# A first batch in a written order on four engines, with idle TensorE products, wider folds and one pool for the feed-forward operands

## The chip, the core and the metric

The kernel runs on one core of one Trainium2 chip. The time is device microseconds of one execution, as the median of three runs. The profile is one more execution, taken by the hardware profiler; its busy times, waits and clock are those of that execution.

Engines are named as in the profile: PE is TensorE, with PEld for its weight loads, DVE is VectorE, ACT is ScalarE, POOL is GpSimd, SP is SyncE, which here only issues DMAs.

## The reference

Eight batches, eight heads, 576 tokens of 64 values a head, 32 pack rows a head, all float32; the two weights come as float64.

```python
def sm_attn(qq, kk, vv):
    s = scale * np.matmul(qq, kk.transpose(0, 1, 3, 2))
    a = np.exp(s - np.max(s, axis=-1, keepdims=True))
    return np.matmul(a / (np.sum(a, axis=-1, keepdims=True) + 1e-09), vv)
p_packed = sm_attn(p, k, v)
x = sm_attn(q, p_packed, p_packed)          # then heads side by side: (8, 576, 512)
...
mixed = np.real(np.fft.fft(np.fft.fft(x, axis=1), axis=2))
u = x + mixed
un = (u - mean(u)) / np.sqrt(var(u) + 1e-06)    # over the 512 values of a token
return u + np.maximum(un @ w_ch1, 0.0) @ w_ch2  # 512 -> 2048 -> 512
```

## The kernel before, in words

**Products in three parts.** Nearly all products are made from operands split in a rounded high part (float32r) and the rest (`hi`, `lo`): `three` (line 240) issues high x high, high x low, low x high into one PSUM bank. A split is a rounding copy on ACT and a subtraction on DVE or POOL (`split`, line 100).

**Two kinds of work.** `front(b)` (line 245) makes one batch's `u`: for each half `g` of the heads, scores `s1` and their exponentials `e1` (letter `s` in the written order), turned by PE transposes (`t`), the packed rows `pp` (`p`), their transposes `ppT`, `pph`, `ppl` (`d`), the second scores `s2` (`q`), maximum and exponentials (`e`), mean and reciprocal (`m`), weights turned by DVE (`a`), the spectrum of the packed rows `gh`, `gl` from products `pg` with a table `basis` (`g`), sums and differences of the tokens `eo`, `f` (`f`, `r`: the folds) and their splits `fh`, `fl`, `xl`, `ol` (`h`). Then products `py`, their splits `yh`, `yl`, `yr`, products `pz` with the tables `tbh`, `tbl`, `tbr`, and products `px`; DVE adds them to `pe`, `qe` and four blocks of 128 tokens of `u` (`ubuf`, line 571). The 64 tokens left of a batch, its block R, go together with the next batch's.

`ffn` (line 659) is the feed-forward part of one tile of up to four blocks of 128 tokens: 16 steps `j`, each with 12 products `ph` (`up`, line 678, 128x512) and 12 products `acc` (`down`, line 695). Between them ACT makes `hh`, and DVE makes `hl` (line 685), which reads the one bank `ph`; so the next step's `ph` waits for `hl`. There are nine tiles, and 3456 such products of 512 columns (24 half-wide ones count as 12). While tile t runs, `front(t+1)` is dealt out over its half steps (`step`, line 776). Tiles 7 and 8 have no front beside them.

**Weights.** float64 chunks of 512 KB are fetched by SP into spare places (`fetch`, line 160) and made float32 by one ACT operation (line 181, "top") and two DVE operations (lines 182 and 183, "bits"). This happens once, in the first batch and in tile 0. Each tile splits all 32 chunks anew, into six buffers `wr`: ACT `wr_h` (line 101) and POOL `wr_l` (line 102).

**What sets the order.** For tiles 1 to 8 the code's order is kept on PE, DVE, ACT and POOL (`tc.manual_schedule`, `MANUAL`). The first batch and tile 0 are left to the tile framework's scheduler, which may reorder them when the program is built. `ORDER[0]` is the order in which the first batch's parts are handed to it; all of `front(0)`, block R too, stands before tile 0. SP's queue brings keys, tables, values, queries and the first weight chunks; the tables come as float32 through a staging place and are split on the chip (`load_base`, `load_tables`, lines 126 to 146).

**Waits between the two.** Tile 0 starts when the blocks of the first batch have been made, less their mean (`un`, line 628, DVE), turned (`untp`, line 635, PE) and split (`uh`, `ul`).

Of the kernel before, what the change touches and what calls it, by code (L numbers as in the profile page):

```python
# [38 lines left out]
ORDER = ("K0 I0 K1 B0 V0 V1 Q0 Q1 W0 W1 W2 W3 s0 t0 p0 d0 s1 t1 p1 q0 e0 d1 g0 q1 e1 m0 m1 a0 f0 r0 h0 a1 "  # L39
         "f1 r1 h1 g1 T0",  # L40
# [38 lines left out]
def tile_kernel(ctx, tc, kpT, qT, v, w1, w2, tabC, tabS, tabR, tabB, tabT, sel, ident_d, out):  # L79
# [3 lines left out]
    cpool = ctx.enter_context(tc.tile_pool(name="cpool", bufs=1))  # L83
    ld = ctx.enter_context(tc.tile_pool(name="ld", bufs=2))
# [15 lines left out]
    def split(hi, lo, src, lo_eng=None):  # L100
        nc.scalar.copy(hi, src)  # L101
        (lo_eng or nc.vector).tensor_tensor(lo, src, hi.bitcast(F32), ALU.subtract)  # L102
# [13 lines left out]
    ubuf = cpool.tile([P, NU, DM], F32, name="ubuf")  # L116
    stages = (STG0 + STG1 * 40)[:2 * NJ]
# [8 lines left out]
    def load_base():  # L126
        nc.sync.dma_start(sels, sel)
        st = load(tabB, [P, 2, N2], "st_base", "wst")
        h = work.tile([P, 2, N2], F32R, tag="tmp", name="base_h", bufs=3)
        nc.scalar.copy(h, st)  # L130
        nc.vector.scalar_tensor_tensor(basis, h.bitcast(F32), selC, st, ALU.mult, ALU.add)
        nc.sync.dma_start(turn, tabT)

    def load_tables():
        for t, d in enumerate((tabC, tabS)):
            st = load(d, [P, 1, KT], "st_tab", (t, 2))
            split(tbh[t], tbl[t], st[:, 0, :])
        st = work.tile([P, 2, 320], F32, tag="wst", name="st_tabr", bufs=2)
        nc.sync.dma_start(st[:101], tabR)
        for t in range(2):  # L140

            h = work.tile([P, DM], F32R, tag="tmp", name="tabr_h", bufs=3)
            nc.scalar.copy(h[:101, :320], st[:101, t, :])
            nc.vector.scalar_tensor_tensor(
                tbr[t][:101], h[:101, :320].bitcast(F32), selA[:101], st[:101, t, :], ALU.mult, ALU.add)
# [3 lines left out]
    sels = cpool.tile([P, 3], F32, name="sels")  # L149
    selA, selB, selC = (sels[:, i:i + 1] for i in range(3))  # L150
# [20 lines left out]
    def load_weights(j):  # L171

        for n, dst in enumerate((w1f, w2f)):
            if (j, n) not in fetched:
                fetch(j, n)
            st = fetched.pop((j, n))
            low, high = st[:, :, 0], st[:, :, 1]
            c = dst[:, j, :].bitcast(I32)


            nc.scalar.activation(c.bitcast(F32), high.bitcast(F32), AF.Prelu, scale=REBIAS, alpha=-2.0 ** 32)  # L181
            nc.vector.tensor_scalar(c, c, 3, None, ALU.logical_shift_left)
            nc.vector.scalar_tensor_tensor(c, low, 29, c, ALU.logical_shift_right, ALU.bitwise_or)
# [30 lines left out]
    def statistics(key):  # L214
        st, u = stat_of[key], u_of[key]
        nc.vector.tensor_scalar(st[:, 1:2], st[:, 0:1], 1.0 / DM, None, ALU.mult)  # L216
        meant[key] = steps[0] or 0

        def squares():
            junk = work.tile([P, DM], F32, tag="tmp", name="junk", bufs=3)  # L220
            nc.scalar.activation(junk, u, AF.Square, bias=st[:, 1:2], scale=-1.0, accum_out=st[:, 2:3])  # L221
# [5 lines left out]
        after(1, squares)  # L227
        after(2, deviation)
# [16 lines left out]
    def front(b):  # L245
# [31 lines left out]
        def scores(*gs):  # L277
# [11 lines left out]
            for g in gs:  # L289
# [31 lines left out]
        def packed(g):  # L321
# [15 lines left out]
            bd = work.tile([P, 4, D], F32, tag="tmp", name="bd", bufs=3)  # L337
            nc.gpsimd.tensor_tensor(bd, pp2[:, 0:1, :].to_broadcast([P, 4, D]),
                                    bmask.unsqueeze(2).to_broadcast([P, 4, D]), ALU.mult)

            def diagonals():
                bdh[g] = work.tile([P, 4 * D], F32R, tag="bdh", name="bdh")
                bdl[g] = work.tile([P, 4 * D], F32R, tag="bdl", name="bdl")
                split(bdh[g], bdl[g], bd.rearrange("p a d -> p (a d)"), nc.gpsimd)

            after(1, diagonals)

        def packed_parts(g):
# [10 lines left out]
            nc.vector.tensor_tensor(lo, tp[:, :P], hi.bitcast(F32), ALU.subtract)  # L359
# [44 lines left out]
        def values_spectrum(g):  # L404
# [6 lines left out]
            for t in range(2):  # L411
# [4 lines left out]
                x = work.tile([P, 2, N2], F32, tag="tmp", name="turned", bufs=3)  # L416
# [17 lines left out]
        def folded(g):
# [42 lines left out]

        def folded_parts(g):
# [3 lines left out]
            fh[g] = work.tile([P, FW], F32R, tag="fh", name="fh")  # L482
            nc.scalar.copy(fh[g], f)  # L483
# [4 lines left out]
            fl[g] = work.tile([P, FW], F32R, tag="fl", name="fl")  # L488
            nc.vector.tensor_tensor(fl[g], f, fh[g].bitcast(F32), ALU.subtract)
# [14 lines left out]
        yh, yl, yr = [], [], []  # L504
        for t, base in enumerate((0, FO)):
# [24 lines left out]
        def spectrum(t, par):  # L530

            pz = bank("pz")
            k0, off = (0, 0) if par is not None else (P, rows.start)
            pars = (0, 1) if par is None else (par,)
            for i, q in enumerate(pars):
                w = slice(KW * q + k0 - off, KW * q + k0 - off + P)
                three(pz[:, :N2], tbh[t][:, w], tbl[t][:, w], yh[t][:, q, :], yl[t][:, q, :], i == 0, False)
            k0 = KW * par if par is not None else k0
            nc.tensor.matmul(pz[:, :N2], tbr[t][:NRC[t], k0 - off:k0 - off + P], yr[t][:NRC[t]], start=False, stop=True)
            sb = work.tile([P, N2], F32, tag=f"spec{t}", name=f"spec{t}", bufs=1)  # L540
            nc.scalar.copy(sb, pz[:, :N2])
            return sb
# [13 lines left out]
        def halves(x):  # L556
            return x.rearrange("p (a c) -> p a c", a=2)
# [335 lines left out]
```

## Time and profile before

| | us |
|---|---|
| median of three runs | 1021.14 (1019.65 to 1021.65) |
| the profiled execution | 1019.84 |
| its span, first to last instruction | 1017.7 |
| PE, DVE, ACT, POOL busy in the span | 967.4, 611.7, 425.3, 469.4 |

A row of the timeline gives start, duration, engine, line, operation, output and inputs, and in square brackets how long the engine had been idle before it and what ended that. PE's rows overlap: a product's row runs from its start to its modelled end, so what a product costs in a row of products is the distance from one start to the next. In the table by stretches each engine has its busy time and, in brackets, its instructions; PEclk is the granted TensorE clock as a share of the full one.

### The profile page before, as it was taken

To read this page: it belongs to the slowest core of one execution; us is meant where nothing else is said; L and a number is where in the kernel's file an instruction comes from. 1 tells how busy PE (TensorE), PEld (TensorE's weight loads), DVE (VectorE), ACT (ScalarE), POOL (GpSimd) and SP (SyncE) were. 2 spreads that over 40 slices of the span, in tenths; PEclk is the share of its full clock that TensorE was granted. 3 is DMA by queue.
4 is the path that set the end of the run, shared out by engine and by line. 5 is a ranking of instruction groups with operands and counts; after the bars stand their busy time and mean duration, and the time that the engine had idled before them with its cause. 6 is when DMAs were issued, how large, how long until landed. Compare 5 with 4: busy or idle time off the path is not lost.

```text
span 1017.7 us, 14984 instructions
## 1 busy us (share of the span) xinstructions
PE 967.4 (95%) x5588; PEld 785.3 (77%) x5588; DVE 611.7 (60%) x1290; ACT 425.3 (42%) x883; POOL 469.4 (46%) x419
## 2 busy tenths in 40 slices
PE   5489879999999999999999999999999999999998
PEld 2457667878877888788877887778778888887886
DVE  4897985558565856577556955595558562323112
ACT  3556444444453444444434435443534343333322
POOL 1535635354445544454355434643455344445443
PEclk9599899999999999999999999999999999999999
DMA  8328440220033002311141112210310110111001
GB/s 327 118 66 290 145 124 1 93 97 22 1 103 129 15 7 84 99 50 42 43 140 50 42 37 99 96 42 21 108 54 21 42 63 1 42 42 41 1 1 42
DMA packets 36462, 72.27 MB, mean 71 GB/s; under 512 B 4161, under 2 KB 17857, under 8 KB 36390
## 3 DMA queue, kind: packets, MB, share of 16 engines
q1 hardware_dynamic: 36390, 71.32, 20.7%
q8 instruction: 44, 0.72, 0.3%
q14 instruction: 28, 0.23, 0.1%
HBM read 55.05 MB, written 16.25 MB: 70 GB/s over the span
## 4 chain that ended last, share of the span: by engine, by line
PE 70%; DVE 14%; issue 7%; POOL 4%; ACT 3%; DMA 1%; ACTq 0%; POOLq 0%; SPq 0%; DVEq 0%
PE ph L678 32%; PE acc L695 26%; POOL wr_l L102 3%; DVE turned L423 1%; PE po L330 1%; PE s L273 1%; DVE hl L685 1%; DVE turned L419 1%; DMA wst<-w 1%; ACT hh L684 1%; PE px L241 1%; PE e1tp L307 1%; PE px L243 1%; PE px L242 1%; DVE ubuf L571 1%
## 5 line engine op out<-in xcount | busy, mean ns | idle before, releaser
L102 POOL TENSOR_TENSOR wr_l<-w1f,wr_h 128x512 fp32r<-128x512 f32 x144 | 191.3, 1330 | 396.5 <-ACT wr_h L101 394.4
L685 DVE SCALAR_TENSOR_TENSOR hl<-ph,hh 128x512 fp32r<-128x512 f32 x144 | 98.6, 685 | 306.5 <-ACT hh L684 306.5
L678 PE MATMUL ph<-uh,wr_h 128*128 128x512 f32 (+1 forms) x580 | 230.8, 398 | 12.9 <-DVE hl L685 10.8
L102 POOL TENSOR_TENSOR wr_l<-w2f,wr_h 128x512 fp32r<-128x512 f32 x144 | 193.3, 1342 | 83.9 <-ACT wr_h L101 83.9
L695 PE MATMUL acc<-wr_l,hh 128*128 128x512 f32 x576 | 225.9, 392 | 4.7 <-POOL wr_l L102 4.7
L678 PE MATMUL ph<-uh,wr_l 128*128 128x512 f32 (+1 forms) x580 | 227.7, 393 | 0.4 <-POOL wr_l L102 0.4
L678 PE MATMUL ph<-ul,wr_h 128*128 128x512 f32 (+1 forms) x580 | 227.6, 392 | 0.2 <-DVE ul L102 0.2
L695 PE MATMUL acc<-wr_h,hh 128*128 128x512 f32 x576 | 226.3, 393 | 0.0
L695 PE MATMUL acc<-wr_h,hl 128*128 128x512 f32 x576 | 225.2, 391 | 0.0
L684 ACT ACTIVATE hh<-ph 128x512 fp32r<-128x512 f32 x144 | 86.0, 597 | 304.3 <-PE ph L678 304.1
L678 PEld LDWEIGHTS ph<-uh,wr_h 128*128 128x128 f32 x580 | 109.9, 189 | 48.5 <-DVE hl L685 9.8
L695 PEld LDWEIGHTS acc<-wr_l,hh 128*128 128x128 f32 x576 | 108.2, 188 | 28.6 <-POOL wr_l L102 7.5
L678 PEld LDWEIGHTS ph<-uh,wr_l 128*128 128x128 f32 x580 | 110.0, 190 | 24.2 <-POOL wr_l L102 0.8
L678 PEld LDWEIGHTS ph<-ul,wr_h 128*128 128x128 f32 x580 | 110.0, 190 | 22.9 <-issue 1.7
L695 PEld LDWEIGHTS acc<-wr_h,hh 128*128 128x128 f32 x576 | 108.3, 188 | 22.8 <-ACT w2f L181 0.8
L695 PEld LDWEIGHTS acc<-wr_h,hl 128*128 128x128 f32 x576 | 108.2, 188 | 22.7
L101 ACT CAST wr_h<-w2f 128x512 fp32r<-128x512 f32 x144 | 89.3, 620 | 9.7 <-PE ph L678 8.1
L101 ACT CAST wr_h<-w1f 128x512 fp32r<-128x512 f32 x144 | 88.4, 614 | 8.1 <-PE ph L678 3.1
L221 ACT ACTIVATE junk<-ubuf,stat 128x512 f32<-128x512 f32 x36 | 25.8, 717 | 61.7 <-DVE stat L216 61.7
L102 POOL TENSOR_TENSOR gl<-turned,gh 128x516 fp32r<-128x516 f32 x16 | 25.2, 1572 | 22.1 <-ACT gh L101 22.1
L241 PE MATMUL py<-gh,fh 128*128 128x258 f32 x64 | 19.2, 307 | 16.4 <-ACT fh L483 15.3
L225 POOL TENSOR_TENSOR stat<-stat,mhalf 128x1 f32<-128x1 f32 x36 | 24.5, 692 | 13.2 <-DVE stat L224 13.1
(203 smaller groups left out, 1285.7 us busy)
## 6 DMA issues: line engine op xcount, KB each, us to landing
kp<-kpT SPq DMA_DIRECT2D x16, 608.0 KB, 5.2
out<-ubuf SPq DMA_DIRECT2D x36, 256.0 KB, 2.1
vt<-v SPq DMA_DIRECT2D x14, 640.0 KB, 4.2
wst<-w SPq DMA_DIRECT2D x17, 512.0 KB, 4.2
qt<-qT SPq DMA_DIRECT2D x14, 576.0 KB, 4.6
far<-unt SPq DMA_DIRECT2D x26, 256.0 KB, 2.0
back<-far SPq DMA_DIRECT2D x104, 64.0 KB, 2.0
ubuf<-w SPq DMA_DIRECT2D x9, 512.0 KB, 4.5
```

Of the source, the lines that this page charges most:

```text
L101: nc.scalar.copy(hi, src)
L102: (lo_eng or nc.vector).tensor_tensor(lo, src, hi.bitcast(F32), ALU.subtract)
L221: nc.scalar.activation(junk, u, AF.Square, bias=st[:, 1:2], scale=-1.0, accum_out=st[:, 2:3])
L225: nc.gpsimd.tensor_tensor(st[:, 2:3], st[:, 2:3], mhalf, ALU.pow)
L241: nc.tensor.matmul(o, lh, rh, start=first, stop=False)
L242: nc.tensor.matmul(o, lh, rl, start=False, stop=False)
L243: nc.tensor.matmul(o, ll, rh, start=False, stop=last)
L273: nc.tensor.matmul(res[g][c][at, :w.stop - w.start], lhs(g, h), rhs(g, h, w), start=True, stop=True, tile_position=(r, h * NPK))
L678: nc.tensor.matmul(ph[:, t], l[:, c * P:(c + 1) * P], r[:, c, t], start=(k == 0), stop=(k == 11))
L684: nc.scalar.activation(hh[:, :T], ph[:, :T], AF.Relu)
L685: nc.vector.scalar_tensor_tensor(hl[:, :T], ph[:, :T], 0.0, hh[:, :T].bitcast(F32), ALU.max, ALU.subtract)
L695: nc.tensor.matmul(acc[i], l[:, w], r, start=(j == 0 and k == 0), stop=(j == NJ - 1 and k == 2))
```

## The change

- **The first batch is written out** on PE, DVE, ACT and POOL and kept in that order (`tc.manual_schedule` around `front(0)` and the turning of the blocks). Deferred pieces have letters of their own in `ORDER[0]`: `x` the exponentials, `b` and `n` the block diagonals, `l` the low part `ppl`, `j` and `J` the joining and the low part of `gh`, `gl`, `F` and `H` the high and low parts of the folds, `w` and `v` the top and the bits of a weight chunk, `z` the first weight split, `P` the products `py` by half `g`, `X` four `px` products made early.
- **Idle products:** `i70` is seven products of a 128x128 zeroed piece of `ubuf` with itself (float32), from no gate; `i122` is twelve from gate 2. A gated group reads a tile as its stationary operand, so that it can't start before that tile is made. There are 59 of them, and nothing reads their results.
- **Half 1's work of the first batch** moves: its weights (`EW`) and its folds (`EF`) from POOL to DVE, and both `gl` from POOL to DVE. `un` of tile 0 goes from DVE to ACT (`turn_blocks`).
- **Wider folds, in all batches:** sums of the even and the odd part go in one operation by a two-step access pattern (`both`): four operations of 128 elements become two of 256, four of 45 two of 90, two copies one.
- **Tables** come already split from the host (`tabH`, `tabL`) by seven DMAs on POOL's queue (`T0` to `T2`).
- **Block R of the first batch**, the squares and the deviations move behind the start of tile 0.
- **Tops of the weights and the first splits of tile 0 keep their place** on ACT (`tc.keep_in_program_order`); otherwise tile 0 is still left to the scheduler.
- **One pool `ffp`**, opened early, holds `uh`, `ul`, `wr`, `hh`, `hl`; the addresses inside it are all alike modulo 2048 bytes.

```diff
-ORDER = ("K0 I0 K1 B0 V0 V1 Q0 Q1 W0 W1 W2 W3 s0 t0 p0 d0 s1 t1 p1 q0 e0 d1 g0 q1 e1 m0 m1 a0 f0 r0 h0 a1 "
-         "f1 r1 h1 g1 T0",
+ORDER = ("K0 K1 V0 I0 Q0 V1 W0 Q1 B0 W1 W2 W3 i70 s0 x0 s1 i40 t0 x1 p0 b0 T0 t1 n0 w0 d0 T1 i20 v0 z0 T2 q0 e0 p1 "
+         "b1 i80 l0 d1 w1 w2 w3 m0 q1 a0 e1 g0 i122 f0 r0 F0 l1 m1 n1 g1 i203 a1 j0 h0 J0 H0 P0 f1 r1 i64 j1 F1 h1 J1 X0 "
...
+    ffp = ctx.enter_context(tc.tile_pool(name="ffp", bufs=2))
...
+    def load_tables(i):
+        todo = [(basis, tabB)] + [x for t in range(2) for x in ((tbh[t], tabH[t]), (tbl[t], tabL[t]), (tbr[t], tabR[t]))]
+        for to, src in (todo[:1], todo[1:3], todo[3:])[i]:
+            nc.gpsimd.dma_start(to, src)
...
     def load_weights(j):
...
+        for n in range(2):
+            tc.keep_in_program_order(top(j, n))
+            bits(j, n)
...
-            e3.tensor_tensor(f[:, 0:128], ec[:, 0:128], ec[:, 144:272], ALU.add)
-            e3.tensor_tensor(f[:, 128:256], ec[:, 0:128], ec[:, 144:272], ALU.subtract)
-            e4.tensor_tensor(f[:, FO:FO + 128], oc[:, 0:128], oc[:, 144:272], ALU.subtract)
-            e4.tensor_tensor(f[:, FO + 128:FO + 256], oc[:, 0:128], oc[:, 144:272], ALU.add)
+            e3.tensor_tensor(both(f, 0, FO + 128, [[1, 128]]), eo[:, :, 0:128], eo[:, :, 144:272], ALU.add)
+            e4.tensor_tensor(both(f, 128, FO, [[1, 128]]), eo[:, :, 0:128], eo[:, :, 144:272], ALU.subtract)
...
+        def idle(n, gate=None):
+            w = gate if gate is not None else ubuf[:, NU - 1, 0:P]
+            for _ in range(n):
+                nc.tensor.matmul(idles[0][:w.shape[-1], :P], w, ubuf[:, NU - 1, 0:P], start=True, stop=True)
+
+        gates = {0: lambda: None, 1: lambda: zs[0], 2: lambda: ms[1], 3: lambda: zs[1], 4: lambda: eos[1][:, 0, 0:P]}
...
+    def turn_blocks(*ks):
+        for i in ks:
+            key = cur.keys[i]
+            cur.un[i] = work.tile([P, DM], F32, tag="ln", name="un")
+            nc.scalar.activation(cur.un[i], u_of[key], AF.Identity, bias=stat_of[key][:, 1:2])
+        for i in ks:
+            for move in cur.moves(i):
+                move()
+
+    with tc.manual_schedule(engines=MANUAL):
+        for at in gen0:
+            if at == "means":
+                turn_blocks(0, 1)
+            elif at == "rest":
+                break
...
-    for _ in gen0:
-        pass
...
-    rest = iter(())
+    rest = gen0
...
-            if t > 0 and i in (0, 2):
+            if i in (0, 2):
                 next(rest, None)
```

The order of the built programs shows it at three places. The first is PE between the spectrum's products `pg` and the first products `py` of the first batch. Before:

```order
L415 MATMUL pg<-basis,ppl 128x258
L413 MATMUL pg<-basis,pph 128x258
L415 MATMUL pg<-basis,ppl 128x258
L241 MATMUL py<-gh,fh 128x258
L242 MATMUL py<-gl,fh 128x258
```

The same place of PE after the change; `m_332` and `z_383` are half 1's maxima and reciprocals, used here as gates:

```order
L442 MATMUL pg<-basis,ppl 128x258
L618 MATMUL idle<-ubuf,m_332 18x128 x12
L440 MATMUL pg<-basis,pph 128x258
L442 MATMUL pg<-basis,ppl 128x258
L440 MATMUL pg<-basis,pph 128x258
L442 MATMUL pg<-basis,ppl 128x258
L618 MATMUL idle<-ubuf,z_383 18x128 x20
L247 MATMUL py<-gh,fh 128x258
L248 MATMUL py<-gl,fh 128x258
L249 MATMUL py<-gh,fl 128x258
```

Where PE had nothing between `pg` and `py`, it now has 32 idle products, in two groups held back by a gate each.

The second place is DVE from the low part of half 1's folds, `fl`, to the first `pe` of the first batch. Before:

```order
L489 TENSOR_TENSOR fl<-f,fh 128x776
L102 TENSOR_TENSOR tbl_91<-w1f,tbh_89 128x448
L102 TENSOR_TENSOR tbl_92<-w2f,tbh_90 128x448
L144 SCALAR_TENSOR_TENSOR tbr_95<-tabr_h,sels,st_tabr 101x320
L144 SCALAR_TENSOR_TENSOR tbr_96<-tabr_h,sels,st_tabr 101x320
L102 TENSOR_TENSOR yl<-py,yh 128x258 x2
L522 SCALAR_TENSOR_TENSOR yr<-yr_h,sels,pyr 101x258
L102 TENSOR_TENSOR yl<-py,yh 128x258 x2
L522 SCALAR_TENSOR_TENSOR yr<-yr_h,sels,pyr 99x258
L564 TENSOR_TENSOR pe<-px,spec_489 128x512
```

The same place of DVE after the change, from half 1's folds on:

```order
L480 TENSOR_TENSOR eo<-a 128x287
L481 TENSOR_TENSOR eo<-a 128x287
L482 TENSOR_TENSOR f<-eo 128x2x128
L483 TENSOR_TENSOR f<-eo 128x2x128
L453 TENSOR_TENSOR turned<-turned 128x258 x2
L530 SCALAR_TENSOR_TENSOR xl<-eo,xh 128x256
L532 TENSOR_TENSOR ol<-eo,oh 128x256
L456 TENSOR_TENSOR gl<-turned,gh 128x516
L536 TENSOR_TENSOR fl<-f,fh 128x776
L107 TENSOR_TENSOR yl<-py,yh 128x258
L604 SCALAR_TENSOR_TENSOR yr<-yr_h,selB,py 101x258
```

The four operations on tables have gone from behind `fl`; ahead of it stand half 1's folds and a `gl`, which were POOL's.

The third place is DVE in the middle of tile 0, before an `hl`. Before:

```order
L182 TENSOR_SCALAR w2f<-w2f 128x512
L423 TENSOR_TENSOR turned<-turned 128x258 x2
L419 TENSOR_TENSOR turned<-pg,turn 128x516 x2
L400 RECIPROCAL z_1209<-z_1209 128x18
L423 TENSOR_TENSOR turned<-turned 128x258 x2
L183 SCALAR_TENSOR_TENSOR w2f<-wst,w2f 128x512
L182 TENSOR_SCALAR w1f<-w1f 128x512
L182 TENSOR_SCALAR w2f<-w2f 128x512
L378 STREAM_TRANSPOSE s_1173<-s2Tt 128x64
L431 STREAM_TRANSPOSE a<-s_1023 128x576
L685 SCALAR_TENSOR_TENSOR hl<-ph,hh 128x512
```

The same part of the second batch's front in tile 0 after the change:

```order
L796 SCALAR_TENSOR_TENSOR hl<-ph,hh 128x512
L447 TENSOR_TENSOR turned<-pg,turn 128x516
L178 TENSOR_SCALAR w1f<-w1f 128x512
L453 TENSOR_TENSOR turned<-turned 128x258 x2
L179 SCALAR_TENSOR_TENSOR w1f<-wst,w1f 128x512
L178 TENSOR_SCALAR w2f<-w2f 128x512
L447 TENSOR_TENSOR turned<-pg,turn 128x516
L179 SCALAR_TENSOR_TENSOR w2f<-wst,w2f 128x512
L447 TENSOR_TENSOR turned<-pg,turn 128x516
L453 TENSOR_TENSOR turned<-turned 128x258 x2
L405 STREAM_TRANSPOSE s_1265<-s2Tt 128x64
L796 SCALAR_TENSOR_TENSOR hl<-ph,hh 128x512
```

The weights' bits (`L178`, `L179`; `L182`, `L183` before) now stand four to a step, between two `hl`, up to the 14th `hl`; before, one step held up to ten and others few or none.

More of the change, by code (lines that the diff above doesn't have):

```diff
@@ L116, in tile_kernel @@
     ubuf = cpool.tile([P, NU, DM], F32, name="ubuf")
+    nc.vector.memset(ubuf[:, NU - 1, 0:P], 0.0)
+    idles = [psf.tile([P, 512], F32, tag="ph", name="idle")]
     stages = (STG0 + STG1 * 40)[:2 * NJ]
@@ L124, in tile_kernel, with load_turn @@
     tbr = [cpool.tile([P, 320], F32R, name=f"tbr{t}") for t in range(2)]
[L126 to L131, printed above, removed]
-        nc.sync.dma_start(turn, tabT)
[L134 to L150, printed above, removed]
+    def load_tables(i):
+        todo = [(basis, tabB)] + [x for t in range(2) for x in ((tbh[t], tabH[t]), (tbl[t], tabL[t]), (tbr[t], tabR[t]))]
+        for to, src in (todo[:1], todo[1:3], todo[3:])[i]:
+            nc.gpsimd.dma_start(to, src)
+    def load_turn():
+        nc.sync.dma_start(selB, sel)
+        nc.sync.dma_start(turn, tabT)
+    selB = cpool.tile([P, 32], F32, name="selB")[:, 0:1]
     fetched = {}
@@ new lines, in front, with spectrum @@
+                 "F": folded_high, "z": lambda _: next(splits)}
+        for x in "xblnjJH":
+            parts[x] = lambda g, x=x: late[x, g]()
+        yh, yl, yr, ypx, spec = [], [], [], {}, {}
+        def spectrum(t, par, tag=None):
+            pz = bank("pz")
+            k0, off = (0, 0) if par is not None else (P, rows.start)
+            pars = (0, 1) if par is None else (par,)
+            for i, q in enumerate(pars):
+                w = slice(KW * q + k0 - off, KW * q + k0 - off + P)
+                three(pz[:, :N2], tbh[t][:, w], tbl[t][:, w], yh[t][:, q, :], yl[t][:, q, :], i == 0, False)
+            k0 = KW * par if par is not None else k0
+            nc.tensor.matmul(pz[:, :N2], tbr[t][:NRC[t], k0 - off:k0 - off + P], yr[t][:NRC[t]], start=False, stop=True)
+            sb = (ffp if tag else work).tile([P, N2], F32, tag=tag or f"spec{t}", name=f"spec{t}", bufs=6 if tag else 1)
+            copied = nc.scalar.copy(sb, pz[:, :N2])
+            if b == 0 and par is None:
+                tc.keep_in_program_order(copied)
+            return sb
@@ L501, in front @@
                 parts[x[0]](int(x[1:] or 0))
[L504 to L505 removed]
+        for t, base in enumerate((0, FO) if b else ()):
             nr = NRC[t]
@@ L649, in wsplits @@
     def wsplits():
-        for _ in tiles:
+        for t, _ in enumerate(tiles):
             for n, j in [(0, 0)] + [x for j in range(1, NJ) for x in ((0, j), (1, j - 1))] + [(1, NJ - 1)]:
-                hi = work.tile([P, DM], F32R, tag="wr", name="wr_h", bufs=6)
-                lo = work.tile([P, DM], F32R, tag="wr", name="wr_l", bufs=6)
-                split(hi, lo, (w1f, w2f)[n][:, j, :], nc.gpsimd)
+                hi = ffp.tile([P, DM], F32R, tag="wr", name="wr_h", bufs=6)
+                lo = ffp.tile([P, DM], F32R, tag="wr", name="wr_l", bufs=6)
+                split(hi, lo, (w1f, w2f)[n][:, j, :], nc.gpsimd, t == 0 and (n or j > 1))
                 ready.append((hi, lo))
```

285 lines of the change are left out of this document (180 added, 105 removed).

## The prediction

> **What bounds the kernel now.** I read the table by stretches first, cut where the first batch's own steps end: at 22.4 us half 0's second scores are turned, at 44.4 the last `fl` is made, at 62.2 tile 0 starts, at 187.3 it ends, and 295.0 ends tile 1.
>
> ```profile
> core 0: us, PE busy (x) PEld busy (x) DVE busy (x) ACT busy (x) POOL busy (x), PEclk, DMA share, GB/s
> 0.00:22.40 22.40, 14.23 (x161) 5.96 (x161) 7.71 (x24) 7.15 (x18) 3.34 (x13) 0.92 0.87 325
> 22.40:44.40 22.00, 5.61 (x27) 4.86 (x24) 18.48 (x43) 10.12 (x19) 12.85 (x31) 0.62 0.47 159
> 44.40:62.20 17.80, 15.49 (x119) 13.08 (x118) 17.47 (x45) 11.96 (x30) 5.04 (x6) 0.90 0.19 52
> 62.20:187.30 125.10, 113.10 (x620) 88.45 (x621) 97.08 (x195) 60.25 (x120) 61.72 (x52) 0.95 0.39 124
> 187.30:295.00 107.70, 107.02 (x650) 87.91 (x649) 72.66 (x157) 47.79 (x101) 48.15 (x42) 1.00 0.18 60
> ```
>
> From 187.3 on PE is busy for 107.02 of 107.70 us at full clock: nothing of this change can shorten that but fewer or cheaper products, and it has neither. So the 830.4 us from 187.3 to the span's end of 1017.7 stay. What can move is the first 187.3 us: 62.2 of head, and a tile 0 of 125.1 us that does about tile 1's work, which takes 107.7. The next two rows, from the instructions of line 741 and from the waits of PE between 60 and 180 us, show where tile 0 ends and what it waits for (us in total, times, longest).
>
> ```profile
> L741 DVE SCALAR_TENSOR_TENSOR ubuf<-acc,stat,ubuf x36: 732/736/752, 187.3 to 1013.9; 128x512 f32<-128x512 f32 x36
> PE ph L678 <- DVE hl L685: 10.1, 4, 4.2
> ```
>
> Of the 17.4 us that tile 0 is longer, 10.1 are these four waits and up to 6.3 the clock (0.05 of 125.1). In the head DVE is the engine that lasts: 18.48 of 22.00 us and 17.47 of 17.80. PE's timeline has its one long hole there, and its clock.
>
> ```profile
> 38.60 0.58 PE L241 MATMUL py<-gh,fh 128*128 128x258 f32 x1 [15.28 <-ACT fh L483]
> ...
> 39.20 0.42 PE L241 MATMUL py<-gh,fh 128*128 128x258 f32 x1
> 39.41 0.42 PE L242 MATMUL py<-gl,fh 128*128 128x258 f32 x1
> ...
> 48.51 0.28 PE L242 MATMUL pz<-yl,tbh 128*128 128x258 f32 x1
> 48.63 0.28 PE L243 MATMUL pz<-yh,tbl 128*128 128x258 f32 x1
> ```
>
> After 15.28 us without work a product of 258 columns costs 0.21 us from start to start, and after 48 us 0.12: the clock came back some 9.5 us after PE had started again. [...]
>
> **The change part by part.** Stretch A, to the end of half 0's turned second scores, 22.4 us. The chain of waits shows an order that costs.
>
> ```profile
> 8.89 1.84 PE s L273 x2
> 10.74 1.04 PE e1tp L307 x4
> 11.78 1.89 PE s L273 x6
> ...
> 15.43 0.83 PE po L330 x40
> 16.26 0.60 PE e1tp L307 x4
> 16.89 0.59 ACT e1T L313
> ...
> 20.13 0.21 PE pptp L352
> ...
> 21.81 0.67 DVE s L378
> ```
>
> Half 0's exponentials are done where this piece begins, at 8.9, but PE first makes half 1's scores at half clock (1.84 and 1.89 us), then waits for half 1's exponentials, and reaches half 0's `po` at 15.43. The written order has both scores ahead of the turning, then half 0 straight through. Seven idle products run from about 1 us until the keys arrive, so I expect full clock by half 0's turning. Counted on from 8.6 (a little of the half-clock scores saved): `e1tp` 0.6, `e1T` 0.6, `po` 0.8, `pp` some 0.4, half 1's `e1tp` and two idle products ahead of `pptp` 0.9, then as before from `pptp` to the end of the turning, 20.13 to 22.48, 2.35; that is 14.3. A weight chunk's two bits operations stand on DVE just there and can cost 0.7: 15.0. So A gains 7.4. Bounds: if all stays at half clock, four idle products (up to 0.45 each by the half-clock rows) and the products add 3, a gain of 4.5; if the bits hide and the clock opens early, 9.
>
> Stretch B, to the last `fl`, 22.0 us, gets longer. ACT's and DVE's rows for the prices, and one of POOL's from the page (busy us and mean ns of one):
>
> ```profile
> 42.62 0.84 ACT L483 CAST fh<-f 128x776 fp32r<-128x776 f32 x1 [3.08 <-POOL f L472]
> 43.49 0.97 DVE L489 TENSOR_TENSOR fl<-f,fh 128x776 fp32r<-128x776 f32 x1 [1.48 <-ACT fh L483]
> 44.37 1.71 DVE L102 TENSOR_TENSOR tbl<-w1f,tbh 128x448 fp32r<-128x448 f32 x1
> 46.00 0.61 DVE L102 TENSOR_TENSOR tbl<-w2f,tbh 128x448 fp32r<-128x448 f32 x1
> 46.54 1.00 DVE L144 SCALAR_TENSOR_TENSOR tbr<-tabr_h,sels,st_tabr 101x320 fp32r<-101x320 f32 x2
> ```
>
> ```profile
> L102 POOL TENSOR_TENSOR wr_l<-w1f,wr_h 128x512 fp32r<-128x512 f32 x144 | 191.3, 1330 | 396.5 <-ACT wr_h L101 394.4
> ```
>
> By columns from `fl` (776 in 0.97) an operation of 576 costs 0.7, of 516 0.65, of 287 0.36; these are estimates. To 18.5 us of DVE work come half 1's weights 0.7 and `eo` 0.7, both `gl` 1.3, and what fell into A before, two `turned` 1.3 and half 1's small `pp` and `ppT`, 0.5; a bits operation and four narrow folds go, some 1.0. That is 22.0. Waits stay: some 0.7 for half 0's exponentials, 1.3 for POOL's subtraction of half 1's mean (the profile page's row above has 1.33 for 512 columns), and `fh` behind POOL's folds, which cost 3.08 before and now lie mostly under the second `gl`, 0.5. That makes 24.5, a loss of 2.5; at best 22.0 (no loss), at worst 29 (a loss of 7) if POOL and DVE hold each other up.
>
> Stretch C, from `fl` to the start of tile 0, 17.8 us. Off DVE go the tables, 1.71, 0.61 and 1.00, some 1.8 of weights, and 1.9 of `un`, which goes to ACT; off PE the half clock, 18 products at 0.09, 1.6. What is left from `fl`: 3.4 until four of six `py` are split and the first two `pz` copied, then on DVE, in order, `pe`, two `qe`, two `ubuf` and two small ones, 2.7 for each of two groups of blocks, then 0.7 for the first `ul`: 9.5. The gain is 8.3, between 6 (DVE held up by POOL's first weight splits) and 10. So tile 0 starts 13.2 us earlier, at 49.0.
>
> Stretch D, tile 0. Its start moves, but do its own waits? The DVE has 97.08 us of work in 125.1, of which much is stretching; two rows of DVE and one of POOL.
>
> ```profile
> 72.80 0.42 DVE L182 TENSOR_SCALAR w2f<-w2f 128x512 int32<-128x512 int32 x1
> ...
> 110.25 1.49 DVE L182 TENSOR_SCALAR w1f<-w1f 128x512 int32<-128x512 int32 x1
> ...
> 109.73 1.72 POOL L102 TENSOR_TENSOR gl<-turned,gh 128x516 fp32r<-128x516 f32 x1
> ```
>
> The same operation takes 0.42 us alone and 1.49 beside a POOL operation, at whose end it ends; the next `hl` stands in the queue behind this one and others, and PE waits its longest 4.2 us. That stretching stays, for POOL's work stays. The written places of the weights spread them: four operations between two `hl` instead of up to ten. I expect more waits, but short ones: 9 us in place of 10.1, and with no hole over 3 us a clock loss of 3 in place of 6.3; block R's six `px` and three DVE operations, now in here, cost 0.4. D gains 4.0. At best the excess falls to some 6 (a gain of 11); at worst the same DVE queue meets PE less favourably (a loss of 4).
>
> The rest: the wider folds in tiles 1 to 7 lie under a busy PE, 0, bounded by the 0.7 us of 107.70 that PE is idle in a tile, a gain of up to 3 in all. The pool moves the feed-forward operands to other addresses, alike modulo 2048 before and after: 0, within 2. Squares, deviations and the `un` on ACT have cover: ACT is busy 60.25 of 125.1. The 59 idle products lie in PE's holes; only those ahead of `pptp` are counted.
>
> The sum, on the profiled execution: 1017.7 - 7.4 + 2.5 - 8.3 - 4.0 = 1000.5, plus the 2.1 by which its own time of 1019.84 exceeds its span, 1002.6. The median of the runs is 1.3 above that execution: **1004.0 us**.
>
> **The rivals.** *Tile 0 comes free of its waits* (0.17): evenly spread weights let `hl` through in time, and D gains 11: 997. For it, DVE's 97.08 us fit under PE's 107.7; against it, the stretching.
>
> *The written order waits more than it saves* (0.18): in a fixed order everything behind a late piece is late. Half 1's chain crosses DVE, POOL and ACT twice, with POOL's folds of half 0 ahead of its subtraction. B then loses 7, and D gains nothing and loses 1: 1004.0 + 4.5 + 5.0 = 1013.5. The 3.08 us that ACT waited for POOL speak for it.
>
> *The weights bind tile 0* (0.04): the start moves and the end doesn't, some 1019 to 1021. The next row, from the waits of SP's queue up to 200 us, is against it:
>
> ```profile
> SPq L237 <- PE s L273: 27.0, 3, 11.7
> ```
>
> The load that holds up the fetches waits for the second batch's scores, which are products of tile 0 and come earlier with it.
>
> *POOL's queue of table loads makes it slower* (0.06). Seven DMAs are now issued by POOL between half 0's `bd`, at about 12 us, and half 1's subtraction of the maximum, which DVE has ready at about 22. No POOL issue is in the trace; one by SP is:
>
> ```profile
> 4.73 0.33 SPq L237 DMA_DIRECT2D w1f<-qT  x1
> ```
>
> With some 3 us of other POOL work there, issues of 0.33 are hidden, and so are 1.0 each. From there on seven times the excess goes into B: at 1.72, the longest POOL row above, 5 us, over a third of the head's gain; from about 3.4 us each it is 17, all of the gain, and beyond that the kernel is slower; at 4, 7 x 3.0 = 21, 1025. [...]
>
> **How the numbers follow.** My forecast, 998 to 1010, has 0.55. With 0.17 for 997, 0.18 for 1013.5, 0.04 for 1020 and 0.06 for 1025, faster by over 0.2% (2 us, about what a measurement of this kernel can tell from no change) has 0.89, within 0.2% 0.05, slower 0.06. The range of 8 in 10 leaves out the slower cases and the far end of the best: 995 to 1016.
>
> **What would show it.** Right: the first `ph` with `ul` at about 49 us, half 0's scores turned at about 15, the last `fl` at about 39.5, PEclk at 1.00 from 10 to 49, tile 0 ending at about 170 with waits for `hl` of under 3 us each, and 107.7 for tile 1. Wrong: POOL without a free moment between 12 and 25 us and DVE waiting for it; PEclk at 0.5 in the head in spite of the idle products; a tile 0 over 125 us; or FFN products with another distance from start to start than before.

## The result and the profile after

Over the runs made together, the changed kernel takes 1009.72 us (median of four, 1008.52 to 1010.87), the kernel before 1020.52 (1019.65 to 1021.65): a ratio of 0.9893, 95% interval 0.9876 to 0.9911. The profiled execution took 1009.1 us, with a span of 1007.3. Faster, as forecast, and within the range, but by 10.8 us instead of 17.1.

The table by stretches of the changed kernel, cut at the same events as before's: half 0's scores turned, last `fl`, first product with `ul`, end of tile 0, end of tile 1.

```profile
core 0: us, PE busy (x) PEld busy (x) DVE busy (x) ACT busy (x) POOL busy (x), PEclk, DMA share, GB/s
0.00:15.70 15.70, 12.96 (x172) 8.84 (x173) 6.11 (x20) 6.35 (x16) 3.80 (x15) 1.00 0.86 325
15.70:41.90 26.20, 19.09 (x145) 14.81 (x143) 22.87 (x46) 9.41 (x17) 11.48 (x27) 0.93 0.70 257
41.90:53.10 11.20, 9.83 (x80) 9.17 (x80) 9.88 (x28) 8.03 (x17) 0.00 (x0) 1.00 0.01 2
53.10:175.30 122.20, 111.18 (x648) 86.93 (x646) 102.70 (x195) 65.04 (x136) 62.84 (x53) 0.99 0.43 130
175.30:283.10 107.80, 107.06 (x651) 88.07 (x650) 72.37 (x147) 47.77 (x101) 49.26 (x43) 1.00 0.18 60
```

A is 6.7 us shorter, B 4.2 longer, C 6.6 shorter, D 2.9 shorter. The rest, from the first instruction of line 852 (741 before) to the end, is 1007.3 - 175.3 = 832.0 instead of 830.4.

```profile
L852 DVE SCALAR_TENSOR_TENSOR ubuf<-acc,stat,ubuf x36: 731/735/752, 175.3 to 1003.2; 128x512 f32<-128x512 f32 x36
```

The waits of PE in tile 0 (us in total, times, longest): those for `hl` are fewer, and those for the weight splits (3.4 us in all) were 0.4 before.

```profile
PE ph L789 <- DVE hl L796: 6.2, 2, 3.2
PE ph L789 <- POOL wr_l L107: 1.5, 1, 1.5
PE acc L806 <- ACT wr_h L104: 1.2, 1, 1.2
PE py L247 <- ACT fh L521: 0.9, 1, 0.9
PE acc L806 <- POOL wr_l L107: 0.7, 1, 0.7
```

Four places of the changed kernel's timeline: half 0's `po` on PE (15.43 us before), its scores turned on DVE, one of POOL's seven table loads with what POOL waited for behind them, and the hand-over to tile 0.

```profile
10.34 0.90 PE L350 MATMUL po<-w1f,e1T 128*32 128x64 f32 x40 [0.57 <-ACT e1T L333]
...
15.00 0.67 DVE L405 STREAM_TRANSPOSE s<-s2T 128x512 f32<-128x512 f32 x1
...
13.82 0.58 POOL L136 DMA_DIRECT2D tbh<-tabH  x1
...
24.15 1.16 POOL L412 TENSOR_TENSOR s<-s,m 128x576 f32<-128x576 f32 x1 [4.44 <-DVE m L411]
...
50.97 1.28 DVE L107 TENSOR_TENSOR ul<-untp,uh 128x512 fp32r<-128x512 f32 x2
...
52.65 0.66 PE L746 MATMUL untp<-ident,un 128*128 128x128 f32 x4
53.06 0.36 PE L789 MATMUL ph<-ul,wr_h 128*128 128x256 f32 x1
```

Seven issues of 0.54 to 0.76 us left POOL idle for 4.44 us afterwards, and no wait of PE in the head ends with one of these loads: they cost nothing that the trace shows. At the hand-over the first product with `ul` stands on PE behind the turning of the last two blocks.

Of the 1.6 us that the rest grew, 1.2 are tile 6, and they come from one wait there. After, DVE and PE:

```profile
781.74 1.58 DVE L716 TENSOR_SCALAR unp<-ubuf,stat 128x512 f32<-128x512 f32 x1
783.35 0.71 DVE L719 STREAM_TRANSPOSE unt<-unp 128x512 f32<-128x512 f32 x1
783.99 0.65 DVE L796 SCALAR_TENSOR_TENSOR hl<-ph,hh 128x512 fp32r<-128x512 f32 x1
784.56 0.52 DVE L498 TENSOR_TENSOR f<-eo 128x90 f32<-128x90 f32 x2
...
784.79 0.47 PE L789 MATMUL ph<-uh,wr_h 128*128 128x512 f32 x1 [1.56 <-DVE f L498]
```

The same place before:

```profile
793.48 0.48 DVE L605 TENSOR_SCALAR unp<-ubuf,stat 128x512 f32<-128x512 f32 x1
793.99 0.71 DVE L608 STREAM_TRANSPOSE unt<-unp 128x512 f32<-128x512 f32 x1
794.62 0.65 DVE L685 SCALAR_TENSOR_TENSOR hl<-ph,hh 128x512 fp32r<-128x512 f32 x1
795.20 1.57 DVE L459 TENSOR_TENSOR f<-eo 128x45 f32<-128x45 f32 x4
```

One operation is stretched in each: `unp` to 1.58 us against 0.48 at 775.58, the four `f` to 1.57 against 0.54 at 786.32. Before, it stood behind the `hl` that PE needs; with the wide folds it is the one ahead of it. (PE's row names `f`, which began last before the wait's end; `ph` does not read it. The `hl` ends at 784.64 us.)

### The profile page after: what moved, and what is told of

It reads as the page before. It is cut to its first block, busy times and chain, and to the rows that moved or that the text cites. A ratio compares the mean times of both kernels' runs of the same rounds, so it can differ in the third digit from the quotient of the medians.

```text
span 1007.3 us, 15127 instructions
## 1 busy us (share of the span) xinstructions
PE 971.7 (96%) x5706; PEld 792.3 (79%) x5706; DVE 610.9 (61%) x1215; ACT 424.6 (42%) x882; POOL 465.7 (46%) x413
## 4 chain that ended last, share of the span: by engine, by line
PE 71%; DVE 13%; issue 7%; POOL 4%; ACT 3%; DMA 1%; ACTq 0%; SPq 0%; POOLq 0%; DVEq 0%
PE ph L789 32%; PE acc L806 27%; POOL wr_l L107 3%; DVE turned L453 1%; DVE turned L447 1%; PE po L350 1%; DVE hl L796 1%; PE s L289 1%; PE px L249 1%; PE px L247 1%; PE px L248 1%; ACT hh L795 1%; PE pz L247 1%; PE e1tp L327 1%; PE py L249 1%
## 5 line engine op out<-in xcount | busy, mean ns | idle before, releaser
L107 POOL TENSOR_TENSOR wr_l<-w2f,wr_h 128x512 fp32r<-128x512 f32 x144 | 195.9, 1361 | 86.0 <-ACT wr_h L104 80.2
L789 PEld LDWEIGHTS ph<-uh,wr_h 128*128 128x128 f32 x580 | 109.3, 188 | 47.0 <-issue 15.4
L789 PEld LDWEIGHTS ph<-ul,wr_h 128*128 128x128 f32 x580 | 109.5, 189 | 21.5 <-issue 0.8
L806 PEld LDWEIGHTS acc<-wr_h,hl 128*128 128x128 f32 x576 | 108.2, 188 | 22.8
L223 ACT ACTIVATE junk<-ubuf,stat 128x512 f32<-128x512 f32 x36 | 25.9, 720 | 55.9 <-DVE stat L218 55.9
L107 POOL TENSOR_TENSOR gl<-turned,gh 128x516 fp32r<-128x516 f32 x14 | 21.8, 1555 | 18.7 <-ACT gh L104 18.7
L453 DVE TENSOR_TENSOR turned<-turned 128x258 f32<-128x258 f32 x32 | 27.5, 898 | 0.5
```

The lines of the kernel that those rows point to most:

```text
L789: nc.tensor.matmul(ph[:, t], l[:, c * P:(c + 1) * P], r[:, c, t], start=(k == 0), stop=(k == 11))
L806: nc.tensor.matmul(acc[i], l[:, w], r, start=(j == 0 and k == 0), stop=(j == NJ - 1 and k == 2))
```

## The experiments

One table for all; the times of stretches are from each run's trace: the start of the first product with `ul`, then from one tile's first instruction of line 852 (or what it is numbered there) to the next tile's. Ratios are to the kernel before.

| kernel | median us | ratio (95%) | tile 0 starts | tile 0 | tiles 2-4 | tiles 5, 6 |
|---|---|---|---|---|---|---|
| before | 1020.52 | | 62.2 | 125.1 | 107.6 | 108.3, 108.2 |
| after | 1009.72 | 0.9893 (0.9876-0.9911) | 53.1 | 122.2 | 107.6 | 108.3, 109.4 |
| e1_no_idle | 1012.74 | 0.9921 (0.9906-0.9937) | 53.5 | 124.8 | 107.6 | 109.5, 109.5 |
| e2_scheduler_order | 1015.73 | 0.9951 (0.9935-0.9967) | 57.3 | 124.6 | 107.6 | 109.4, 109.5 |
| e3_narrow_folds | 1007.32 | 0.9876 (0.9858-0.9893) | 51.7 | 122.3 | 107.6 | 108.3, 108.2 |
| e4_old_pool | 1020.06 | 0.9994 (0.9982-1.0006) | 53.2 | 124.4 | 108.9 | 109.4, 109.4 |
| a5_all_plus_32 | 1011.68 | 0.9907 (0.9892-0.9921) | 53.3 | 122.7 | 107.6 | 109.5, 109.5 |
| a6_unlike_512 | 1010.81 | 0.9902 (0.9887-0.9916) | 52.8 | 123.0 | 107.6 | 109.5, 109.4 |
| a9_unlike_448 | 1019.83 | 0.9991 (0.9978-1.0003) | 52.7 | 123.1 | 108.9 | 109.3, 109.4 |
| a10_same_residues | 1019.13 | 0.9989 (0.9979-0.9999) | 53.0 | 123.6 | 108.7 | 109.3, 109.3 |
| m7_tile0_written | 1025.07 | 1.0035 (1.0022-1.0048) | 52.5 | 137.4 | 107.6 | 109.4, 109.5 |
| m8_no_keep | 1021.35 | 1.0002 (0.9992-1.0013) | 58.0 | 130.5 | 107.6 | 109.4, 109.4 |
| b11_narrow_early_weights | 1010.14 | 0.9901 (0.9885-0.9917) | 52.3 | 124.6 | 107.6 | 108.2, 108.2 |
| b12_narrow_uneven_weights | 1009.99 | 0.9896 (0.9877-0.9914) | 52.4 | 124.5 | 107.5 | 108.3, 108.2 |

**The idle products.**

```diff
-        parts["i"] = lambda x: idle(x // 10, gates[x % 10]())
+        parts["i"] = lambda x: None
```

> The changed kernel without its 59 idle products; all else is kept. Theory (the idle products hold the clock that the head needs): PE starts its clock with the first scores at about 8.6 us, half 0's scores are turned some 2 to 3 us later than 15.7, and part of the py and pz products falls into half clock again, 1 to 2 us; tile 0 starts at about 56 instead of 53.1, and the time is 3 to 5 us above the changed kernel's 1009.7: 1013 to 1015. Rival (the head is set by DVE, ACT and POOL, and PE has time to spare at half clock too): tile 0 starts within 1 us of 53.1, 1009 to 1011.

The table by stretches of this run:

```profile
8.00:39.00 31.00, 16.29 (x154) 10.00 (x151) 25.47 (x59) 13.20 (x30) 13.40 (x27) 0.56 0.84 310
39.00:53.50 14.50, 11.98 (x96) 10.92 (x94) 11.50 (x31) 8.88 (x18) 1.23 (x6) 1.00 0.01 2
```

The idle products do hold the clock: without them it is at half from 11.3 to 38.6 us, with them only from 23.6 to 27.0 in that stretch. But half 0's scores are turned at 16.3 instead of 15.7, and tile 0 starts 0.4 us later. For the head the rival is right: DVE's 25.47 of 31 us and the waits set it, not PE. The median is 3.0 us higher all the same. Tile 0 is 2.6 longer, and tile 5 has the longer form that a5 and a6 show with their idle products; the two intervals overlap. Against a5 and a6 the difference is 1.1 and 1.9 us. How much of the 3.0 is the idle products' doing stays open.

**The written order.**

```diff
-    with tc.manual_schedule(engines=MANUAL):
+    with nullcontext():
```

(around the first batch only)

> The changed kernel with the first batch left to the scheduler again; its parts, idle products, moved work and tables are kept. Theory (the written order itself carries the gains of A and C): half 1's scores come before half 0's turning again, tile 0 starts at 58 or later, and the time is 5 us or more above 1009.7. Rival (the gain comes from the work that left DVE, the tables and un, and the order is only a frame): tile 0 starts within 2 us of 53.1, 1008 to 1012.

Slower by 6.0, and neither theory as put. A stays good (16.1): handing the parts over in the new order is enough for it. What is lost is in C: 14.3 us instead of 11.2, for the scheduler lets weight chunks in between (the bits of 4 chunks are made before tile 0's start, against 2 in after). What the work that left DVE is worth, the tables, `un` and block R, no run shows: none took it back.

**The pins.** The same change with the weights' tops and tile 0's first splits left to the scheduler:

```diff
-            tc.keep_in_program_order(top(j, n))
+            top(j, n)
...
-                split(hi, lo, (w1f, w2f)[n][:, j, :], nc.gpsimd, t == 0 and (n or j > 1))
+                split(hi, lo, (w1f, w2f)[n][:, j, :], nc.gpsimd)
```

> The changed kernel without the pinned places of the weights' tops and of tile 0's first splits on ACT; the scheduler may take them as early as it likes. Theory (pinning cut the lead of the weights to 4 to 7 us, which is where the new waits for wr come from, 3.4 us in tile 0): the waits for wr_l and wr_h go, but four to ten bits operations collect again ahead of some hl, whose waits grow to the 10 us of before; tile 0 within 3 us of 122.2. Rival (pinning only costs): tile 0 takes 118 to 119, 1006.

11.6 us slower than after: all of the gain. Before tile 0's start stand 13 tops instead of 4, and the bits of 9 chunks instead of 2; B takes 30.0 us instead of 26.2, C 12.4 instead of 11.2. On DVE the bits lie between the last steps of the head (timeline of this run):

```profile
50.03 0.42 DVE L662 TENSOR_TENSOR qe<-px,spec 128x256 f32<-128x256 f32 x1
50.36 0.68 DVE L179 SCALAR_TENSOR_TENSOR w2f<-ubuf,w2f 128x512 int32<-128x512 int32 x1
50.96 0.68 DVE L665 SCALAR_TENSOR_TENSOR ubuf<-qe,pe 128x512 f32<-128x512 f32 x1
```

The waits for `wr` in tile 0 shrink to 0.8 us, as expected, those for `hl` grow to 8.2 in 3, and the clock there falls to 0.92. My bound of 3 us on tile 0 was far too small.

**Tile 0 in the code's order.**

```diff
-        with tc.manual_schedule(engines=MANUAL) if t > 0 else nullcontext():
+        with tc.manual_schedule(engines=MANUAL):
```

> The changed kernel with tile 0 too kept in the code's order on PE, DVE, ACT and POOL, where the scheduler had it. Theory (D's 14 us above a free tile come from the order that the scheduler gave DVE between two hl): the waits for hl, 6.2 us in 2, fall below 3, tile 0 takes 115 to 119 us instead of 122.2, 1003 to 1007. Rival (it is the amount of work, DVE's 102.7 of 122.2 us with POOL beside it, so any order waits): within 2 us of 1009.7, the waits only spread over more places; or slower, where a weight split or a transpose is then met too early.

My theory fell. The scheduler's tile 0 is 15 us better than the code's; the waits of PE between 52 and 190 us say where:

```profile
PE py L247 <- ACT fh L521: 8.2, 2, 7.9
PE ph L789 <- DVE hl L796: 4.2, 2, 3.2
PE s L289 <- ACT e L316: 3.7, 1, 3.7
```

The second batch's products stand on PE at fixed places here, ahead of feed-forward products, which do not read the `fh` that PE waits for.

**The folds.** The kernel with the narrow folds of before in all batches:

```diff
-            e3.tensor_tensor(both(f, 0, FO + 128, [[1, 128]]), eo[:, :, 0:128], eo[:, :, 144:272], ALU.add)
-            e4.tensor_tensor(both(f, 128, FO, [[1, 128]]), eo[:, :, 0:128], eo[:, :, 144:272], ALU.subtract)
+            e3.tensor_tensor(f[:, 0:128], ec[:, 0:128], ec[:, 144:272], ALU.add)
+            e3.tensor_tensor(f[:, 128:256], ec[:, 0:128], ec[:, 144:272], ALU.subtract)
...
```

> The changed kernel with the narrow folds of before in all batches (four operations of 128 elements, four of 45, two copies). Theory (the wide folds save no time on DVE, 1.79 us a half against 1.75, and only shift what meets POOL's splits): tile 6's wait of 1.56 us ahead of ph goes, tile 6 takes 108.2 instead of 109.4, and the time is 1 to 2 us below 1009.7. Rival (the wide folds shorten B and every front): 1 to 3 us above 1009.7.

The fastest of all, 2.4 us below after. The two intervals overlap, but the traces show two gains. Tiles 5 and 6 take 108.3 and 108.2; the six other runs with wide folds and untouched products (e1, e2, a5, a6, m7, m8) have 109.4 or more in both, and after in one. And B is a little shorter: 25.7 to 26.0 us in the three runs with narrow folds, 26.2 to 26.7 in the seven with wide folds and the same head; but e1, with wide folds and no idle products, has 25.9 too. (The rest of the earlier start is A, which ends between 14.8 and 15.8 in these runs.) In after, POOL's part of the folds begins only behind DVE's last `f`:

```profile
36.51 0.43 DVE L483 TENSOR_TENSOR f<-eo 128x256 f32<-128x256 f32 x1
...
37.11 0.94 POOL L498 TENSOR_TENSOR f<-eo 128x90 f32<-128x90 f32 x2 [6.16 <-DVE f L483]
...
40.90 0.97 DVE L536 TENSOR_TENSOR fl<-f,fh 128x776 fp32r<-128x776 f32 x1 [1.62 <-ACT fh L521]
```

With narrow folds it begins behind `eo`, beside DVE's:

```profile
34.88 0.45 DVE L481 TENSOR_TENSOR eo<-a 128x287 f32<-128x287 f32 x1
35.13 1.21 POOL L498 TENSOR_TENSOR f<-eo 128x45 f32<-128x45 f32 x4 [5.63 <-DVE eo L480]
...
39.55 0.97 DVE L534 TENSOR_TENSOR fl<-f,fh 128x776 fp32r<-128x776 f32 x1 [1.00 <-ACT fh L519]
```

A pattern of two steps spans nearly all of `f`, so two engines that write different parts of it now wait for one another. Nor is a wide operation cheaper: in tile 6 from the first `f` to `unp` it was 785.51 to 787.26 before, 1.75 us, and 773.79 to 775.58 after, 1.79. The narrow ones overlap there (0.28 us long, 0.20 to 0.21 from start to start); the wide ones do not (0.43 long, 0.46 apart).

**The pool.** First the old one:

```diff
-    ffp = ctx.enter_context(tc.tile_pool(name="ffp", bufs=2))
...
     work = ctx.enter_context(tc.tile_pool(name="work", bufs=2))
+    ffp = work
```

> The changed kernel with uh, ul, wr, hh, hl and the two early spectra in the general pool as before, at other addresses. Theory (the addresses don't matter): tiles 1 to 5 take 107.5 to 107.7 as now, and the time is within 0.7 us of 1009.7. Rival (equal alignment shortens the products or their loads): the FFN products lie further apart and each full tile takes 0.2 us or more longer, 1011 or more.

10.3 us slower, all of the gain once more, and the rival is right: tiles 1 to 5 take 1.1 to 1.4 us longer each, tiles 7 and 8, which have no front, 1.8 and 1.9. The groups of PE between 300 and 600 us (busy us, mean ns):

```profile
L789 PE MATMUL ph<-ul,wr_h 128*128 128x512 f32 x178 | 70.3, 395 | 0.0
...
L806 PE MATMUL acc<-wr_h,hl 128*128 128x512 f32 x177 | 69.7, 394 | 0.0
```

After has 390 for both. From start to start it is 0.232 us here and 0.227 there (medians). In this build `wr` lies at 1632 modulo 2048 and `uh`, `ul`, `hh`, `hl` at 32; in after all lie at 1408, and before all lay at 1920. Four kernels part the possible reasons.

```diff
...
-    selB = cpool.tile([P, 32], F32, name="selB")[:, 0:1]
+    selB = cpool.tile([P, 40], F32, name="selB")[:, 0:1]
```

> The changed kernel with every feed-forward operand 32 bytes further on: wr, uh, ul, hh, hl all lie at 1440 modulo 2048 instead of 1408, so still alike, but at 32 modulo 64 as in the run with the old pool. Theory (what counts is that each address is a multiple of 64): the full tiles take 108.8 to 109.1 us as with the old pool, and the time is about 1020. Rival (what counts is that they are alike): the tiles keep 107.5 to 107.7, and the time stays at 1009 to 1011.

107.6: an odd multiple of 32 does no harm while all are alike. (96 bytes behind the pool kept the other tiles at multiples of 128 from where they were.)

```diff
+        gap = ffp.tile([P, 128], F32, tag="gap", name="gap", bufs=1)
...
         cur.parts(0)
```

> The changed kernel with 512 bytes between wr and the other four: wr stays at 1408 modulo 2048, uh, ul, hh and hl lie at 1920, so unlike modulo 2048, but all are multiples of 128. Theory (multiples of 64 are what counts): tiles of 107.5 to 107.7, 1009 to 1011. Rival (alike modulo 2048 is what counts): tiles of 108.8 to 109.1, about 1020.

107.6 again: they need not be alike. With these two, both of my theories for the old pool had fallen.

```diff
+        gap = ffp.tile([P, 112], F32, tag="gap", name="gap", bufs=1)
...
         cur.parts(0)
```

> The changed kernel with 448 bytes between wr and the other four: wr at 1408, uh, ul, hh and hl at 1856 modulo 2048, the distance that they had with the old pool, but all multiples of 64. Theory (the distance is what counts, and 512 was a harmless one): tiles of 108.8 to 109.1, about 1020. Rival (it takes this distance and an odd multiple of 32 together, or something else of the old pool): tiles of 107.5 to 107.7, 1009 to 1012.

108.9, products of 395 ns:

```profile
L789 PE MATMUL ph<-ul,wr_h 128*128 128x512 f32 x180 | 71.1, 395 | 0.0
...
L806 PE MATMUL acc<-wr_h,hl 128*128 128x512 f32 x176 | 69.5, 395 | 0.0
```

The distance does it, without the odd multiple of 32: 448 bytes between `wr` and the others cost what the old pool cost, 512 nothing. The fourth kernel has that gap and `selB` 224 bytes longer, which gives the old pool's own places:

> The changed kernel with exactly the old pool's places modulo 2048: wr at 1632, uh, ul, hh and hl at 32; only the multiples of 2048 differ, and the other tiles keep their pool. Theory (the places modulo 2048 made the old pool slow): tiles of 108.8 to 109.1 and products 0.232 us apart instead of 0.227, about 1020. Rival (something else of that run: how far apart the operands lie, or a pool shared with the rest): tiles of 107.5 to 107.7, 1009 to 1012.

108.7, the same. So it is where the operands lie to each other, not the pool. The gap moves the tiles of the later pools as well, but with the old pool `e1`, `a`, `f` and `yh` lay where they lie in after, modulo 2048, and the products were slow all the same.

**Where tile 0's waits come from.** Two tries on the narrow folds, each a list of half steps in place of every second one:

```diff
...
-            if t == 0 and i % 2 == 0 and i // 2 + LEAD < NJ:
-                load_weights(i // 2 + LEAD)
+            if t == 0 and i in WHEN:
+                load_weights(WHEN.index(i) + LEAD)
```

> The changed kernel with narrow folds, and with the weight chunks of tile 0 made one step earlier from the second half step on (chunks 2, 3, 4 at half steps 0, 1, 2, then one every second half step). Theory (the late waits of tile 0, 4.7 us for hl and 4.9 us for wr, come from weights that were cut to a lead of 4 to 7 us, while the first 45 us of the tile have DVE time to spare): the waits for wr go and those for hl shrink, tile 0 takes 116 to 119 us instead of 122.3, 1002 to 1005. Rival (only three staging places: the fetch of the next chunk waits for the bits of an earlier one, and the lead is lost again by the tile's middle): tile 0 stays within 2 us of 122.3, 1006 to 1009.

The theory of the lead fell: the waits for `hl` stay at 4.7 us, those for `wr` are 6.4 instead of 4.9, and tile 0 takes 2.3 us more than in e3. With narrow folds, the steps from 98 to 135 us look like this:

```profile
98.10:107.50 9.40, 7.46 (x42) 4.76 (x42) 9.37 (x14) 3.94 (x7) 6.97 (x6) 1.00 0.42 126
107.50:116.30 8.80, 5.60 (x26) 4.34 (x24) 8.70 (x15) 5.14 (x10) 3.52 (x3) 1.00 0.56 199
116.30:125.10 8.80, 7.32 (x25) 5.60 (x25) 8.80 (x20) 2.79 (x6) 7.07 (x8) 0.81 0.42 125
125.10:135.40 10.30, 8.29 (x42) 6.55 (x43) 9.57 (x29) 4.35 (x9) 5.30 (x2) 1.00 0.31 102
```

DVE is full there (36.4 of 37.3 us), and the longest waits of both kinds fall into them. So the last run took two chunks out.

> The changed kernel with narrow folds, and with tile 0's weight chunks dealt out unevenly: chunks 2 to 10 at half steps 0, 2, 3, 5, 6, 8, 10, 11, 13, chunk 11 at 16, then 20, 22, 24, 26. The four steps from 98 to 135 us, in which DVE was busy for 36.4 of 37.3 us with narrow folds, have two chunks to make instead of four; the five steps before, in which it had 0.2 to 1.5 us a step to spare, have two more. Theory (the waits of tile 0 come from DVE being full in those four steps, not from the lead): the waits for hl, 4.7 us, and for wr, 4.9 us, fall by 4 to 6 us together, tile 0 takes 116 to 119 us, 1001 to 1004. Rival (DVE has no real room earlier, or the fetches with three staging places can't follow): new waits in the first 45 us of the tile eat the gain, tile 0 within 2 us of 122.3, 1006 to 1009.

Nearer the rival again, and a little worse than it said (2.2 us more than e3 in tile 0). The longest wait for `hl` falls from 3.2 to 2.9 us, but there are more of them, earlier too:

```profile
PE ph L788 <- DVE hl L795: 5.2, 4, 2.9
PE acc L805 <- POOL wr_l L108: 1.8, 2, 1.1
PE s2T L290 <- DVE turned L448: 1.5, 1, 1.5
```

That DVE is full where PE waits is shown; that taking weights from there shortens the tile is not. What would is open.

## Why the prediction was right, and where its sizes were off

- **A, predicted 15.0, measured 15.7.** As put, half 0 no longer waits behind half 1: its `po` starts at 10.34 us instead of 15.43, and at 10.25 without the idle products (e1). That this comes from the order of the parts is read from these rows; no run had the old order back. The clock, which my working counted on, hardly matters: with half clock from 11.3 us on (e1) A is 16.3, not the 3 us more of my worst case. That half 1's scores of before ran at half clock I read from their lengths, 1.91 and 1.93 us (at 8.82 and 11.71) against 1.04 for products of the same shape at 21.40; PEclk reads 1.00 at all three.
- **B, predicted a loss of 2.5, measured 4.2.** DVE waits for 2.7 us in this stretch, my sum had 2.5, but that is luck: POOL's subtraction cost it 0.2 instead of 1.3, and `fh` 1.6 instead of 0.5, for POOL's folds end at 39.99 us, behind the second `gl` (39.27). The term that was too small is DVE's work, 22.0: it is 26.2 - 2.7 = 23.5. I had priced it by rows of operations alone, but half 1's weights took 1.32 us beside POOL instead of half 0's 0.72, and the wide folds saved nothing: with narrow ones B is 0.2 to 1.0 us shorter, not longer.

```profile
21.84 0.72 DVE L465 TENSOR_TENSOR s<-s,z 128x576 f32<-128x576 f32 x1
...
30.24 1.32 DVE L465 TENSOR_TENSOR s<-s,z 128x576 f32<-128x576 f32 x1 [0.19 <-POOL s L428]
...
30.23 0.72 POOL L107 TENSOR_TENSOR bdl<-bd,bdh 128x256 fp32r<-128x256 f32 x1
```

- **C, predicted 9.5, measured 11.2.** My 3.4 to the first `pe` was 3.5 and my 2.7 for each group of blocks 2.8. The rest, "0.7 for the first `ul`", was 2.1: two `ul` in a row, and PE's fixed order with the turning of blocks 2 and 3 ahead of the product.
- **D, predicted 4.0, measured 2.9.** The sum is near, its terms are not, and this too is luck. The waits for `hl` fell by 3.9 us, to 6.2, where I had put 1.1, though both that are left are over 3 us. The clock was at half for 3.4 us of the tile instead of 13.7, which by half of these times is some 5 us gained instead of 3.3. I had put it down to there being no hole over 3 us, a condition that no run shows: through a hole of 3.2 us the clock stayed at 1.00, and it fell to 0.50 at the end of one of 3.0. Against these 9 us stand two terms, as estimates. The waits for `wr` grew by 3.0, which I had put at nothing. And PE has 28 products more in this stretch (648 against 620): block R's six, 0.7 us instead of my 0.4, and some 1.2 us of the second batch's first scores, which before ran ahead of tile 0 (the row below is of the kernel before). That leaves some 4; for the last 1 us I have no account. The cause named was the written places of the weights. Without the pins (m8) tile 0 takes 8.3 us more than after and 5.4 more than before; but m8 also fills the head with bits, so what of the 2.9 is theirs stays open. One reading was wrong: the stretched bits operation of before ended at 111.74 us, not with POOL's at 111.45 but 0.3 behind it.

```profile
58.62 1.04 PE L273 MATMUL s<-kp 64*32 64x512 f32 x8
```

- **The rest, predicted unchanged, measured 1.6 longer.** I had bounded the wide folds on the side of a gain alone. In tile 6 they moved a stretched operation ahead of an `hl`.
- **The pool, predicted 0 within 2.** Right between these two kernels, as both keep the distance at zero. But the pool is worth 10 us to the new one: back in the general pool its operands would lie 448 bytes apart.
- **The rivals.** POOL's issues took 0.54 to 0.76 us: far from 3.4. The written order "waits more than it saves" only in B, by 4.2 us.

Undone one at a time, idle products, order, pins and pool cost 3.0, 6.0, 11.6 and 10.3 us, together three times the gain of 10.8: pins and pool keep away losses that the kernel before, with its operands at like places and the bits of 2 chunks ahead of tile 0, did not have.

## What to carry to other kernels

An order that is written out holds only what is inside it: ask what else the scheduler may move in, and pin that too. When buffers move, compare where the two operands of the frequent products lie to each other. Fewer, wider operations are no gain until a row shows it, above all when their patterns cover what another engine writes.

## What the runs showed of the hardware

- Products of 512 columns take 394 to 402 ns a row (group means between 300 and 600 us) where the weights' tile and the other operand lie 448 bytes apart modulo 2048 (e4, a9, a10), and tiles 2 to 4 take 108.7 to 108.9 us. At distances of 0 (after) and 512 (a6) they take 390 to 397 ns, and these tiles 107.6 us. From start to start it was 0.232 us in e4 and 0.227 in after. Distances of 0 and 512 are alike modulo 512 as well, so the runs do not say which modulus counts. Which distances do harm beyond 448 wasn't tried, and why it does is open.
- In tile 0 of the changed kernel the clock was at half from 126.0 to 129.4 us, from the end of a hole of PE of 3.0 us (123.29 to 126.31) on. Through a hole of 3.2 us nine us earlier (114.42 to 117.60) it stayed at 1.00, so the length of a hole alone does not decide it; what does is open. In the kernel before the clock took 9.5 us to come back after PE had started again at 38.60; in the head of the changed one it took 2.9 (24.06 to 27.0).
